# Column sums of the first weights from a column of ones behind a slab of raw x, and one product moved from VectorE to GpSimd

**Chip, cores, metric.** One core of one Trainium2 chip. The metric is the time of the kernel on the device in microseconds (us), median of several executions. The span of the profile is about 1.8 us shorter than the reported time of the same execution. In each call of the experiments one execution of the kernel before lay well above its others (206.99, 205.27, 204.94 and 204.81 us). Only the first, over 1.5% above the fastest, is left out of the ratios; the other three widen their intervals and make the ratios of those calls about 0.1% lower than the medians would.

## The reference

```python
x  = A_x                                  # 1 x 2048 x 640, bf16
xn = layernorm(x)                         # over the 640 columns, no affine part
s  = irfft2(rfft2(xn) * (w_r + 1j*w_i))   # spectral filter, to bf16
g  = silu((gelu(xn @ w_gate) * (xn @ w_up)) @ w_down)   # 640 -> 1536 -> 640
return x + s * g
```

## The kernel before

The kernel does not write its instructions in a fixed order. It collects tasks, each with engines it may run on, a cost, a rank and what it comes after, and a list scheduler of its own ("the plan") runs through them on estimated times. The order in which the plan starts tasks is the order in which they are put on the queue of each engine. Each engine then works through its queue strictly in order, whatever the real times are.

```python
# the plan: when a task may start (cut)
for s in t.new:                     # t needs a free buffer of this tag
    mine = self.slots[s.tag]
    k = len(mine) - self.bufs[s.tag] + ...
    if k >= 0:
        for u in mine[k].users:
            if u.done is None:
                return None
            at = max(at, u.done + self.MARGIN[e])       # MARGIN: PE 250 ns, others 60

BUFS = dict(sp=2, pg=2, pu=2, ..., mc=2, Y=1, R=2, IU=2, ..., xr=3, ...)   # slots per tag
```

TensorE must start before the row statistics of the layer norm are there. So the first two tiles of gate and up work on raw x, turned slab by slab (a slab is 128 rows), and are corrected later: (x - m) r W = r (x W - m colsum(W)). This needs the column sums of the first weights. Before, they are 20 matmuls against a column of ones:

```python
def turn_raw(n1):                       # slabs 0..3 of raw x
    ...                                 # five 128x128 transposes on TensorE, then a copy:
    raw[n1] = add(lambda e: copy_on(e, XR[:, :, n1 * P:(n1 + 1) * P], ...),
                  {"ACT": c_act(640), "DVE": (415, 560)}, ...)
    if n1 < 2:
        k, w, got = ((0, Wg, g_in), (1, Wu, u_in))[n1]
        def sums(e, t):
            for c in range(5):
                nc.tensor.matmul(pt.tile[:, 1, 256 + t:257 + t], lhsT=w[:, c, t*P:t*P+P], rhs=ones, ...)
        ss = [add(..., "PE", (132, 370), (0, 4, k, t), after=[got[t], raw[n1]], ...) for t in range(2)]
        sums_out[k] = add(... copy to WSUM[:, 2*k:2*k+2] ...)

# the corrections of the first two tiles, when RB (row statistics, broadcast to all partitions) has landed
m = add(... nc.vector.scalar_tensor_tensor(out=ev, in0=RB[:, 1], scalar=WSUM[...], in1=ev, mult, add) ...)
normed.append(add(... nc.vector.tensor_tensor(out=ev, in0=ev, in1=RB[:, 0], op=mult) ...))
a = add(gelu of the gate tile, "ACT", ...)
u_done = add(product of both, "DVE", ...)
```

Three other parts matter, none of which the change edits:

```python
def turn_dma(n1, ap):                   # slabs 4..15 of normalised x: a DMA transpose on SyncE's queue
    turned[n1] = add(nc.sync.dma_start_transpose(out=xnT[...], in_=sxn...), "SP", ..., rank (0, 0, n1))

def fold(j, aps):                       # first transform of slabs 2j, 2j+1
    ..., A = ..., Slot("mc")            # only two buffers of this tag
    # two casts PSUM -> A (ScalarE or VectorE), then a store on SyncE's queue:
    stored[j] = dma(D2[:, 2*j:2*j+2, :], A, ...)

def load_res(n1):                       # x again, for the residual at the very end
    nc.gpsimd.dma_start(out=xr_slot, in_=xv[:, n1, :])   # on GpSimd's own queue; three slots
```

Of the kernel before, what the change touches and what calls it, by code (L numbers as in the profile page):

```python
# [11 lines left out]
FP32 = mybir.dt.float32  # L12
# [102 lines left out]
class Plan:  # L115
# [21 lines left out]
    def ready(self, t, e, now):  # L137
# [8 lines left out]
        for s in t.new:  # L146
            mine = self.slots[s.tag]
            k = len(mine) - self.bufs[s.tag] + more.get(s.tag, 0)
            more[s.tag] = more.get(s.tag, 0) + 1
            if k >= 0:  # L150
                for u in mine[k].users:
                    if u.done is None:
                        return None
                    at = max(at, u.done + self.MARGIN[e])
# [68 lines left out]
def kernel(  # L223
# [37 lines left out]
    ones = consts.tile([P, 1], BF16)  # L261
    WSUM = consts.tile([P, 4], FP32)
    XR = persist.tile([P, 5, 512], BF16)
# [89 lines left out]
    nc.gpsimd.memset(ones, 1.0)  # L353
# [101 lines left out]
    def turn_raw(n1):  # L455
        pt = Slot("sp")

        def half():
            return pt.tile[:, 0, :].bitcast(BF16)[:, 0:D]
# [6 lines left out]
        if n1 == 0:  # L466
            keep_warm(2, [a], (0, 0, 0))
        raw[n1] = add(lambda e: copy_on(e, XR[:, :, n1 * P:(n1 + 1) * P], half().rearrange("p (c n) -> p c n", c=5)),
                      {"ACT": c_act(640), "DVE": (415, 560)}, None, (0, n1), after=[a], use=[pt], hold=200)
        if n1 < 2:  # L470
            k, w, got = ((0, Wg, g_in), (1, Wu, u_in))[n1]

            def sums(e, t):
                for c in range(5):
                    nc.tensor.matmul(pt.tile[:, 1, 256 + t:257 + t], lhsT=w[:, c, t * P:t * P + P], rhs=ones, start=(c == 0), stop=(c == 4), skip_group_check=True)
            ss = [add(lambda e, t=t: sums(e, t), "PE", (132, 370), (0, 4, k, t), after=[got[t], raw[n1]], use=[pt]) for t in range(2)]
            sums_out[k] = add(lambda e: copy_on(e, WSUM[:, 2 * k:2 * k + 2], pt.tile[:, 1, 256:258]), {"ACT": c_act(2), "DVE": c_dve(2, 1, True)}, None, (0, -1), after=ss, use=[pt])
# [96 lines left out]
    t = add(rows_pe, "PE", (215, 460), (0, 7), after=[*minused] + [roots[n1] for n1 in range(4)], new=[sr])  # L574
    t = add(lambda e: nc.vector.tensor_copy(out=place(rt, (P,), FP32)[0:8, :], in_=sr.tile[0:8, 0, 0:P]), "DVE", c_dve(128, 1, True), (1, 3, 0.7), after=[t], new=[rt], use=[sr])
# [305 lines left out]
    def gate_up(grp, t):  # L881
# [4 lines left out]
        for k, (w, ps, wt) in enumerate(((Wg, pg, g_in[t]), (Wu, pu, u_in[t]))):  # L886
            parts = [(128 * j, 128 * j + 128) for j in range(4)] if grp == 0 and t < 3 else [(0, 512)]
            mm = []
            for lo, hi in parts:
                def go(e, w=w, ps=ps, lo=lo, hi=hi):  # L890
                    if lo == 0:
                        place(ps, (512,))
                    for c in range(5):
                        nc.tensor.matmul(ps.tile[:, lo:hi], lhsT=w[:, c, t * P:(t + 1) * P],  # L894
                                         rhs=XR[:, c, lo:hi] if early else xnT[:, c, grp * 512 + lo:grp * 512 + hi], start=(c == 0), stop=(c == 4),
                                         skip_group_check=True)
# [4 lines left out]
                              after=[wt] + mm[-1:] + [got[n] for n in range((grp * 512 + lo) // P, (grp * 512 + hi) // P)],  # L901
                              new=[ps] if lo == 0 else [], use=[] if lo == 0 else [ps]))
            last[id(w)] = mm[-1]
# [16 lines left out]
        for k, (w, ps) in enumerate(((Wg, pg), (Wu, pu))):  # L920
# [4 lines left out]
                                                                         op0=ALU.mult, op1=ALU.add), "DVE", c_dve(512, 1), (0, 100), after=[out, rb_in, sums_out[k]], use=[ev])  # L925
            normed.append(add(lambda e, ev=ev: nc.vector.tensor_tensor(out=four(ev), in0=four(ev), in1=RB[:, 0], op=ALU.mult), "DVE", c_dve(512, 1), (0, 100), after=[m], use=[ev]))
# [128 lines left out]
```

## Time and profile before

| | before |
|---|---|
| median of 6 runs (range) | 202.90 us (202.82 to 203.20) |
| span of the profile | 201.2 us |
| TensorE busy | 195.1 us (97%) |
| TensorE's last matmul starts | 197.04 us |
| GpSimd busy | 32.1 us |

The busy shares and the chain stand in the prediction below. First SyncE's queue of the kernel before, in the timeline (start in us, time to issue, engine, line, operation, tiles), then ScalarE's casts of the last two folds in the same stretch. SyncE only issues; the transfer lands later.

```profile
48.84 0.54 SPq L304 DMA_DIRECT2D D<-mc  x1
49.47 1.24 SPq L505 DMA_TRANSPOSE xnT<-s  x1
50.77 0.57 SPq L304 DMA_DIRECT2D T<-tab_t  x1
...
53.12 0.69 ACT L297 CAST mc<-sp 128x640 bf16<-128x640 f32 x1
54.25 0.69 ACT L297 CAST mc<-sp 128x640 bf16<-128x640 f32 x1 [0.44 <-PE sp L542]
```

The first line is the store of the sixth fold: it goes ahead of the last DMA transpose and of a table of 512 KB (T). By the last of its sixteen completions in the trace it lands at 51.55. The last fold's casts need the same mc buffer; they start at 53.12 and wait for nothing but TensorE.

Second, ScalarE at the second corrected tile: the activation of a streamed gate tile (`ge<-pg`) stands ahead of the one of the corrected tile (`ge<-IU`).

```profile
36.50 0.58 ACT L907 ACTIVATE ge<-pg 128x512 bf16<-128x512 f32 x1
36.97 0.62 ACT L907 ACTIVATE ge<-IU 128x512 bf16<-128x512 f32 x1
```

### The profile page before, as it was taken

How to read it: one execution, taken by the hardware profiler on the slowest of the kernel's cores; microseconds unless marked ns; L12 is line 12 of the kernel's file. 1: busy time of each engine (PE TensorE's matmuls, PEld its weight loads, DVE VectorE, ACT ScalarE, POOL GpSimd, SP SyncE). 2: the span in 40 equal slices, each digit the busy share in tenths (PEclk: the TensorE clock that was granted, in tenths of full speed). 3: DMA queues.
4: the chain of work that ended last, by engine and by line, in shares of the span. 5: the costliest groups of instructions: out<-in, count | busy, mean ns of one | idle time of the engine just before them, and what ended most of it. 6: DMA issues, size and time to landing. Idle time of an engine off the chain costs nothing.

```text
span 201.2 us, 4145 instructions
## 1 busy us (share of the span) xinstructions
PE 195.1 (97%) x1530; PEld 118.2 (59%) x1547; DVE 147.7 (73%) x314; ACT 128.9 (64%) x230; POOL 32.1 (16%) x70
## 2 busy tenths in 40 slices
PE   7999999999999999999999999999999999999992
PEld 3994444677544555677755555467765555457781
DVE  3579879999323249999998999933257788888774
ACT  3999699965632768778775766333466565766421
POOL 2413133699100000000000000000001122211210
PEclk9999999999999999999999999999999999999999
DMA  6999999798994947865244210116701243332422
GB/s 175 327 315 324 342 388 213 157 140 201 161 320 152 367 125 158 214 143 190 61 128 122 77 47 21 65 49 224 317 0 47 86 129 103 101 104 92 134 99 65
DMA packets 35894, 32.62 MB, mean 162 GB/s; under 512 B 10910, under 2 KB 32930, under 8 KB 35874
## 3 DMA queue, kind: packets, MB, share of 16 engines
q1 hardware_dynamic: 34434, 29.49, 50.6%
q0 software_dynamic: 1152, 2.66, 6.1%
q10 hardware_dynamic: 288, 0.20, 0.5%
q8 instruction: 12, 0.20, 0.4%
q14 instruction: 8, 0.07, 0.1%
HBM read 22.51 MB, written 9.19 MB: 158 GB/s over the span
## 4 chain that ended last, share of the span: by engine, by line
PE 94%; DMA 2%; ACT 1%; issue 1%; DVE 1%; SPq 0%; DVEq 0%
PE pu L894 26%; PE pg L894 25%; PE pg L972 13%; PE pu L972 13%; PE sp L706 3%; PE sp L839 3%; PE sp L781 2%; PE sp L815 2%; DMA X<-in_A_x_dram 2%; PE sp L541 2%; PE sp L679 2%; PE sp L699 1%; PE sp L833 1%; PE sp L487 1%; PE sp L542 0%
## 5 line engine op out<-in xcount | busy, mean ns | idle before, releaser
L894 PE MATMUL pu<-xnT,Wu 128*128 128x512 bf16 (+1 forms) x237 | 56.7, 365 | 0.5
L894 PE MATMUL pg<-xnT,Wg 128*128 128x512 bf16 (+1 forms) x236 | 56.3, 365 | 0.4
L911 DVE TENSOR_TENSOR uT<-pu,ge 128x512 bf16<-128x512 f32 x46 | 31.7, 690 | 21.9 <-PE pu L894 18.3
L972 PEld LDWEIGHTS <-uT 128*128 128x128 bf16 x396 | 37.9, 98 | 13.5
L907 ACT ACTIVATE ge<-pg 128x512 bf16<-128x512 f32 x46 | 27.5, 598 | 24.4 <-PE pg L894 23.5
L894 PEld LDWEIGHTS <-Wg 128*128 128x128 bf16 x285 | 25.1, 98 | 22.4 <-issue 0.2
L894 PEld LDWEIGHTS <-Wu 128*128 128x128 bf16 x285 | 25.0, 98 | 21.8
L972 PE MATMUL pg<-Wd,uT 128*128 128x320 bf16 (+2 forms) x204 | 30.7, 293 | 0.0
L935 POOL DMA_DIRECT2D xr<-in_A_x_dram x16 | 8.8, 549 | 133.8 <-DVE res L959 133.8
L297 ACT CAST ma<-sp 128x644 bf16<-128x644 f32 (+1 forms) x32 | 23.4, 792 | 9.7 <-PE sp L839 7.9
L972 PE MATMUL pu<-Wd,uT 128*128 128x320 bf16 (+1 forms) x192 | 29.5, 297 | 0.0
L981 ACT ACTIVATE th<-pu 128x320 f32<-128x320 f32 (+1 forms) x16 | 7.0, 435 | 10.7 <-PE pu L972 10.1
L297 ACT CAST IU<-sp 128x640 bf16<-128x640 f32 x16 | 10.9, 691 | 4.2 <-PE sp L781 4.1
L297 ACT CAST Vt<-sp 128x640 bf16<-128x640 f32 x16 | 10.8, 691 | 3.7 <-PE sp L815 3.7
L981 ACT ACTIVATE th<-pg 128x320 f32<-128x320 f32 (+2 forms) x17 | 7.3, 430 | 9.2 <-PE pg L972 8.5
L986 DVE SCALAR_TENSOR_TENSOR G<-th,pg 128x320 bf16<-128x320 f32 (+1 forms) x16 | 7.7, 480 | 7.1 <-ACT th L981 7.1
L986 DVE SCALAR_TENSOR_TENSOR G<-th,pu 128x320 bf16<-128x320 f32 (+1 forms) x16 | 7.7, 480 | 5.4 <-ACT th L981 5.1
L297 ACT CAST mc<-sp 128x640 bf16<-128x640 f32 x16 | 10.6, 703 | 1.3 <-PE sp L542 1.3
L434 POOL TENSOR_TENSOR RSTD<-MVA,mh 128x1 f32<-128x1 f32 x12 | 8.9, 743 | 6.6 <-DVE MVA L416 5.9
L419 ACT ACTIVATE th<-X 128x640 bf16<-128x640 bf16 x11 | 8.1, 738 | 1.6 <-DMA D<-th 1.6
L857 DVE TENSOR_TENSOR mb<-ma 128x640 bf16<-128x640 bf16 x8 | 3.9, 492 | 7.0 <-ACT ma L297 7.0
L759 DVE TENSOR_TENSOR R<-Y 64x644 bf16<-64x644 bf16 x16 | 7.8, 490 | 0.4
(107 smaller groups left out, 246.6 us busy)
## 6 DMA issues: line engine op xcount, KB each, us to landing
BU<-D SPq DMA_DIRECT2D x8, 640.0 KB
D<-mc SPq DMA_DIRECT2D x8, 320.0 KB
xr<-in_A_x_dram POOLq DMA_DIRECT2D x16, 160.0 KB, 2.7
D<-IU SPq DMA_DIRECT2D x8, 320.0 KB
out_dram<-res SPq DMA_DIRECT2D x15, 160.0 KB
Wg<-in_B_w_gate_dram SPq DMA_DIRECT2D x6, 320.0 KB
Wu<-in_B_w_up_dram SPq DMA_DIRECT2D x6, 320.0 KB
Wd<-in_B_w_down_dram SPq DMA_DIRECT2D x6, 320.0 KB
```

The source lines that it names most:

```text
L297: return nc.scalar.copy(out=out, in_=in_) if e == "ACT" else nc.vector.tensor_copy(out=out, in_=in_)
L419: nc.scalar.activation(out=place(junk, (D,)), in_=x, func=ACT.Copy, scale=-1.0 / D, accum_out=less)
L434: nc.gpsimd.tensor_tensor(out=rstd, in0=var, in1=mh, op=ALU.pow)
L706: nc.tensor.matmul(into(q, ri), lhsT=sZ.tile[:, q, ri, :], rhs=FM[:, kinds[q][2] + (4 if ri and kind == 0 else 0), :], start=False, stop=T ...
L759: nc.vector.tensor_tensor(out=o, in0=Yf[:, ::-3, :], in1=Yf[:, 1:3, :], op=ALU.subtract)
L894: nc.tensor.matmul(ps.tile[:, lo:hi], lhsT=w[:, c, t * P:(t + 1) * P], rhs=XR[:, c, lo:hi] if early else xnT[:, c, grp * 512 + lo:grp * 51 ...
L907: nc.scalar.activation(out=ge.tile, in_=pg.tile if src is None else src, func=ACT.Gelu_apprx_tanh)
L911: nc.vector.tensor_tensor(out=u.tile, in0=pu.tile if src is None else src, in1=ge.tile, op=ALU.mult)
L935: nc.gpsimd.dma_start(out=sx.tile, in_=xv[:, n1, :])
L972: nc.tensor.matmul(ps.tile[:, 0:hi - lo], lhsT=uT[grp, ks[i]].tile[:, j * P:(j + 1) * P], rhs=Wd[:, ks[i], lo:hi], start=(i == 0), stop=(i ...
L981: nc.scalar.activation(out=th.tile[:, 0:hi - lo], in_=ps.tile[:, 0:hi - lo], func=ACT.Tanh, scale=0.5)
L986: nc.vector.scalar_tensor_tensor(out=G2.tile[:, lo:hi], in0=th.tile[:, 0:hi - lo], scalar=1.0, in1=ps.tile[:, 0:hi - lo], op0=ALU.add, op1 ...
```

## The change

The intent: no matmuls of their own for the column sums. A column of ones stands in the turned x, behind slab 0, so the matmuls of slab 0 are one column wider and yield the sums in column 128 of pg and pu. With it, VectorE gives the second product of the up corrections to GpSimd, the row statistics are fetched with a higher rank, the plan's rule for buffers handed on within TensorE becomes less cautious, and the plan holds ScalarE free longer for the copy of slab 1 (`hold`, 1000 ns in place of 200). Line numbers shift: L894 becomes L886, L972 L968, L297 L296, L304 L303, L505 L496, L907 L903, L911 L907, L924 L920, L926 L922.

```diff
@@ the plan @@
-                    at = max(at, u.done + self.MARGIN[e])
+                    at = max(at, u.start + u.engs[e][0] if u.on == e == 'PE' else u.done + (self.MARGIN[e] if now > 9000 else 60))
@@ tiles @@
-    ones = consts.tile([P, 1], BF16)
-    XR = persist.tile([P, 5, 512], BF16)
+    XR = persist.tile([P, 5, 513], BF16)
-    nc.gpsimd.memset(ones, 1.0)
+    nc.gpsimd.memset(XR[:, :, 128:129], 1.0)
@@ turn_raw: the sums go, the copies of slabs 0 and 1 stay on ScalarE @@
-        raw[n1] = add(lambda e: copy_on(e, XR[:, :, n1 * P:(n1 + 1) * P], ...
+        raw[n1] = add(lambda e: copy_on(e, XR[:, :, n1 * P + (n1 > 0):(n1 + 1) * P + (n1 > 0)], ...
-                      {"ACT": c_act(640), "DVE": (415, 560)}, ..., hold=200)
+                      {"ACT": c_act(640)} if n1 < 2 else {"ACT": c_act(640), "DVE": (415, 560)}, ..., hold={1: 1000}.get(n1, 200))
-        if n1 < 2:
-            ... (the 20 one-column matmuls and their two copies)
@@ rows (statistics of slabs 0 to 3 on their way to RB) @@
-    t = add(rows_pe, "PE", (215, 460), (0, 7), after=[*minused] + [...], new=[sr])
+    t = add(rows_pe, "PE", (215, 460), (0, 7), after=[*minused, turned[2]] + [...], new=[sr])
-    ... "DVE", c_dve(128, 1, True), (1, 3, 0.7), after=[t] ...
+    ... "DVE", c_dve(128, 1, True), (0, 3.5), after=[t] ...
@@ gate_up, first two tiles @@
-                        nc.tensor.matmul(ps.tile[:, lo:hi], lhsT=..., rhs=XR[:, c, lo:hi] if early else ...
+                        more = early and lo == 0
+                        nc.tensor.matmul(ps.tile[:, lo:hi + more], lhsT=..., rhs=XR[:, c, lo + (lo > 0):hi + 1 if lo or more else hi] if early else ...
+                if early and lo == 0:
+                    sums_out[k, t] = add(... copy_on(e, WSUM[:, 2 * k + t:2 * k + t + 1], ps.tile[:, 128:129]), {"DVE": ...}, ...)
+                    mm.append(sums_out[k, t])
@@ corrections @@
-            normed.append(add(... nc.vector.tensor_tensor(out=four(ev), in0=four(ev), in1=RB[:, 0], op=ALU.mult), "DVE", ...
+            normed.append(add(... (nc.gpsimd if e == "POOL" else nc.vector).tensor_tensor(...), *(("POOL", (1700, 1800), (1, 8)) if k else ("DVE", ...)) ...
```

More of the change, by code (lines that the diff above doesn't have):

```diff
@@ L467, in turn_raw @@
             keep_warm(2, [a], (0, 0, 0))
-        raw[n1] = add(lambda e: copy_on(e, XR[:, :, n1 * P:(n1 + 1) * P], half().rearrange("p (c n) -> p c n", c=5)),
-                      {"ACT": c_act(640), "DVE": (415, 560)}, None, (0, n1), after=[a], use=[pt], hold=200)
-        if n1 < 2:
-            k, w, got = ((0, Wg, g_in), (1, Wu, u_in))[n1]
-            def sums(e, t):
-                for c in range(5):
-                    nc.tensor.matmul(pt.tile[:, 1, 256 + t:257 + t], lhsT=w[:, c, t * P:t * P + P], rhs=ones, start=(c == 0), stop=(c == 4), skip_group_check=True)
-            ss = [add(lambda e, t=t: sums(e, t), "PE", (132, 370), (0, 4, k, t), after=[got[t], raw[n1]], use=[pt]) for t in range(2)]
-            sums_out[k] = add(lambda e: copy_on(e, WSUM[:, 2 * k:2 * k + 2], pt.tile[:, 1, 256:258]), {"ACT": c_act(2), "DVE": c_dve(2, 1, True)}, None, (0, -1), after=ss, use=[pt])
+        raw[n1] = add(lambda e: copy_on(e, XR[:, :, n1 * P + (n1 > 0):(n1 + 1) * P + (n1 > 0)], half().rearrange("p (c n) -> p c n", c=5)),
+                      {"ACT": c_act(640)} if n1 < 2 else {"ACT": c_act(640), "DVE": (415, 560)}, None, (0, n1), after=[a], use=[pt], hold={1: 1000}.get(n1, 200))
     for n1 in range(4):
@@ L573, in rows_pe @@
         nc.tensor.transpose(out=place(sr, (2, 512))[0:8, 0, 0:P], in_=RM.rearrange("p k n -> p (k n)"), identity=identF)
-    t = add(rows_pe, "PE", (215, 460), (0, 7), after=[*minused] + [roots[n1] for n1 in range(4)], new=[sr])
-    t = add(lambda e: nc.vector.tensor_copy(out=place(rt, (P,), FP32)[0:8, :], in_=sr.tile[0:8, 0, 0:P]), "DVE", c_dve(128, 1, True), (1, 3, 0.7), after=[t], new=[rt], use=[sr])
+    t = add(rows_pe, "PE", (215, 460), (0, 7), after=[*minused, turned[2]] + [roots[n1] for n1 in range(4)], new=[sr])
+    t = add(lambda e: nc.vector.tensor_copy(out=place(rt, (P,), FP32)[0:8, :], in_=sr.tile[0:8, 0, 0:P]), "DVE", c_dve(128, 1, True), (0, 3.5), after=[t], new=[rt], use=[sr])
     rs = dma(D5, lambda: rt.tile[0:8, :], (0, -5, 0), 4096, after=[t], use=[rt])
@@ L893, in go @@
                     for c in range(5):
-                        nc.tensor.matmul(ps.tile[:, lo:hi], lhsT=w[:, c, t * P:(t + 1) * P],
-                                         rhs=XR[:, c, lo:hi] if early else xnT[:, c, grp * 512 + lo:grp * 512 + hi], start=(c == 0), stop=(c == 4),
+                        more = early and lo == 0
+                        nc.tensor.matmul(ps.tile[:, lo:hi + more], lhsT=w[:, c, t * P:(t + 1) * P],
+                                         rhs=XR[:, c, lo + (lo > 0):hi + 1 if lo or more else hi] if early else xnT[:, c, grp * 512 + lo:grp * 512 + hi], start=(c == 0), stop=(c == 4),
                                          skip_group_check=True)
@@ L900, in gate_up @@
                 mm.append(add(go, "PE", c_pe(*[hi - lo] * 5), rk,
-                              after=[wt] + mm[-1:] + [got[n] for n in range((grp * 512 + lo) // P, (grp * 512 + hi) // P)],
+                              after=[wt] + mm[-2:] + [got[n] for n in range((grp * 512 + lo) // P, (grp * 512 + hi) // P)],
                               new=[ps] if lo == 0 else [], use=[] if lo == 0 else [ps]))
+                if early and lo == 0:
+                    sums_out[k, t] = add(lambda e, k=k, ps=ps: copy_on(e, WSUM[:, 2 * k + t:2 * k + t + 1], ps.tile[:, 128:129]),
+                                         {"DVE": c_dve(1, 1, True)}, None, (0, -1), after=[mm[-1]], use=[ps])
+                    mm.append(sums_out[k, t])
             last[id(w)] = mm[-1]
@@ L924, in gate_up @@
             m = add(lambda e, ev=ev, k=k: nc.vector.scalar_tensor_tensor(out=four(ev), in0=RB[:, 1], scalar=WSUM[:, 2 * k + t:2 * k + t + 1], in1=four(ev),
-                                                                         op0=ALU.mult, op1=ALU.add), "DVE", c_dve(512, 1), (0, 100), after=[out, rb_in, sums_out[k]], use=[ev])
-            normed.append(add(lambda e, ev=ev: nc.vector.tensor_tensor(out=four(ev), in0=four(ev), in1=RB[:, 0], op=ALU.mult), "DVE", c_dve(512, 1), (0, 100), after=[m], use=[ev]))
+                                                                         op0=ALU.mult, op1=ALU.add), "DVE", c_dve(512, 1), (0, 100), after=[out, rb_in, sums_out[k, t]], use=[ev])
+            normed.append(add(lambda e, ev=ev: (nc.gpsimd if e == "POOL" else nc.vector).tensor_tensor(out=four(ev), in0=four(ev), in1=RB[:, 0], op=ALU.mult), *(("POOL", (1700, 1800), (1, 8)) if k else ("DVE", c_dve(512, 1), (0, 100))), after=[m], use=[ev]))
         a = add(lambda e: act(e, evs[0].tile), "ACT", c_act(512), (0, 100), after=normed[:1], new=[ge], use=evs[:1])
```

## The prediction

> **What bounds the kernel now.** I read the page's busy shares first, then the chain of work that ended last, then busy time by stretch, and last the order of instructions in the first 8 us and around 30 to 40 us, which is all that the change touches.
>
> ```profile
> PE 195.1 (97%) x1530; PEld 118.2 (59%) x1547; DVE 147.7 (73%) x314; ACT 128.9 (64%) x230; POOL 32.1 (16%) x70
> ...
> PE 94%; DMA 2%; ACT 1%; issue 1%; DVE 1%; SPq 0%; DVEq 0%
> ```
>
> TensorE (PE) is busy for 195.1 of the 201.2 us span, and the chain is TensorE for 94%. So I ask of each part of the change only: does it take time from TensorE's stream, or open a gap in it? In which stretch, the next view says (after the count of the window: busy us and instructions of each engine, then clock, DMA share, GB/s).
>
> ```profile
> 5.26:7.30 2.04, 1.94 (x41) 1.82 (x40) 0.65 (x2) 2.04 (x5) 0.64 (x2) 1.00 1.10 321
> 7.30:12.60 5.30, 5.30 (x101) 5.30 (x99) 3.74 (x11) 5.05 (x13) 2.23 (x6) 1.00 1.16 326
> 12.60:40.00 27.40, 27.30 (x174) 14.71 (x173) 24.88 (x56) 25.51 (x59) 9.88 (x19) 1.00 1.06 288
> ```
>
> From 7.30 us on the first column has no room: 5.30 of 5.30 and 27.30 of 27.40. I also took every start-to-start distance of the matmuls and subtracted N/2.4 ns. After 7 us the only excess over 100 ns that is not a missing record (those are all 218 ns, one 512-column matmul) is 121 ns at 39.38 us. TensorE streams from 7 us to its last matmul at 197.0 us, and the 4.2 us after that are a tail of ScalarE, VectorE and one store. So the time is: when TensorE starts to stream, plus its work, plus the tail. The change can only touch the first two. The stretch in question:
>
> ```profile
> 4.28 1.06 PE L369 MATMUL sp<-uT 128*128 128x512 bf16 x2
> ...
> 5.26 0.27 PE L475 MATMUL sp<-ones,Wg 128*128 128x1 bf16 x5
> ...
> 5.40 0.60 PE L464 MATMUL sp<-ident,X 128*128 128x128 bf16 x5
> ...
> 5.83 0.27 PE L475 MATMUL sp<-ones,Wg 128*128 128x1 bf16 x5
> ...
> 5.96 1.25 PE L894 MATMUL pg<-XR,Wg 128*128 128x128 bf16 x15
> 6.03 0.69 ACT L297 COPY XR<-sp 128x640 bf16<-128x640 bf16 x1
> ...
> 7.05 0.39 PE L475 MATMUL sp<-ones,Wu 128*128 128x1 bf16 x10
> ...
> 7.31 0.44 PE L464 MATMUL sp<-ident,X 128*128 128x128 bf16 x5
> ```
>
> The second number is duration, and matmuls overlap, so I read starts: the ten one-column matmuls of Wu hold TensorE from 7.05 to 7.31, 25.4 ns each. The fifteen matmuls at 5.96 hide a gap: the last five of them start only at 6.78, when the ScalarE copy of slab 1 (6.03 + 0.69 = 6.72) is done; TensorE stood still for 0.26 us. There are 0.13 us more ahead of 5.26. By the last of the sixteen completions of each transfer, slab 1 of x landed at 5.21, the first Wu at 6.60, slab 2 at 7.07, slab 3 at 7.55.
>
> **What the Trainium skill says.** "TensorE: Matmul & The Clock Gate", section "Wait — 56ns, not 53.3ns?": a matmul takes N/1.2 ns cold, N/2.4 + 2.5 ns warm, and never less than about 25 ns from start to start. The trace agrees: 25.4 ns for one column, 56 for 128, and 107 for the cold transposes before 5.8 us. A column more in a 128-column matmul is therefore 0.4 ns; a matmul of its own is 25. "PSUM — Partial Sum Buffer", section "PSUM bank collisions raise a hardware error": TensorE must not write a bank while another engine reads it. So the copy of a sum out of the bank of pg or pu holds up the next slab's matmuls into that bank. The kernel before shows no such wait (its sums had a bank of their own). "GPSIMD Engine Reference", section "3.1 Elementwise — side-by-side cycle accounting": a two-input fp32 product is 1.96 times VectorE's at 2048 elements. The trace before has no GpSimd product of this size. "SBUF — State Buffer", section "Who interferes with whom": GpSimd reading SBUF contends with a VectorE instruction of two SBUF inputs, and one blocks the other whole. The trace fits: GpSimd's 128x1 power takes 0.55 us in calm stretches and 2.24 us at 40.57 us, amid back-to-back VectorE tensor_tensors.
>
> **The change part by part.**
> 1. Removed: 20 one-column matmuls with their weight loads. Starts: 5.264 to 5.396, 5.833 to 5.961, 7.052 to 7.306, that is 0.132 + 0.128 + 0.254 = 0.51 us of TensorE. Added: one column in 20 matmuls, 20 x 0.42 ns = 0.01 us.
> 2. How much of the 0.51 us is gained? The 0.254 us of the Wu sums stand after the last gap, in the stream: all of it. The 0.26 us of the Wg sums stand ahead of the gap that ends at 6.78. That end is set by slab 1's copy, which follows slab 1's transposes, which follow its landing at 5.21 at the cold clock; I let the copy end where it did, so the removal would only widen the gap. But the first Wu is there at 6.60, and its slab 0 products can now go first, at about 6.66 in place of 6.78: 0.12 us. Gain 0.25 + 0.12 = 0.37 us.
> 3. Moved: two ScalarE copies of the sums (0.164 us each by the view of that tile) become four on VectorE of one column each; by the 0.15 us of its smallest instruction (L416) some 0.6 us. VectorE is busy for only 0.65 of 2.04 and 3.74 of 5.30 us here, so that is not the bound.
> 4. Added wait: matmul, sum copy, next matmul of the same bank. A matmul shows 0.22 us; ScalarE began 0.04 us after the last transpose's end (4.485 to 4.52), and TensorE 0.06 us after a copy's end (6.72 to 6.78). With a 0.15 us copy: 0.22 + 0.04 + 0.15 + 0.06 = 0.47 us between the starts, where a free stream has 0.06. Four times 0.41 us would be 1.6 us if nothing stood between. The plan knows of the dependence and has transposes and the other three banks' slabs to put there, 0.28 us each, so most is filled. I charge 0.1 us, for a VectorE queue in which a statistics instruction (0.45 us) that waits for a landing stands ahead of a copy.
> 5. GpSimd takes the last up product. Here are the four instructions of the corrections (durations are minimum, median, maximum):
>
> ```profile
> L924 DVE SCALAR_TENSOR_TENSOR IU<-RB,WSUM,IU x2: 743/744/746, 29.8 to 34.1; 128x512 f32<-128x512 f32 x2
> L924 DVE SCALAR_TENSOR_TENSOR R<-RB,WSUM,R x2: 743/744/745, 30.4 to 34.8; 128x512 f32<-128x512 f32 x2
> L926 DVE TENSOR_TENSOR IU<-IU,RB x2: 679/680/681, 31.7 to 36.0; 128x512 f32<-128x512 f32 x2
> L926 DVE TENSOR_TENSOR R<-R,RB x2: 681/682/684, 32.3 to 36.6; 128x512 f32<-128x512 f32 x2
> ```
>
> VectorE loses 2 x 0.68 us; GpSimd gains 2 x 1.34 us by the page's ratio (an estimate; the plan books 1.7). The results are wanted by the down product's second half: its matmuls start at 39.94 us, and the last corrected tile is ready at 38.92 (38.24 + 0.68). That is 1.0 us of slack against 0.66 to 1.0 us more latency, and the row statistics are now fetched with more urgency: before, their broadcast landed at 29.43 and the first correction ran at 29.78. I expect that fetch about 1 us earlier and no gap. Zero.
> 6. The plan's rule for buffers reused within TensorE, and its smaller margin early on, change the order only. In a stream without gaps that is worth zero.
>
> Sum: -0.25 - 0.12 + 0.01 + 0.10 = -0.26 us. From 202.86 that is 202.6; since some of the retuning may close part of the 0.39 us of early gaps, I take 202.5.
>
> **The rivals.**
> - The sum copy's round trip becomes the wait. For it: four new links from TensorE to VectorE and back, each 0.41 us if bare. Against: VectorE is half idle there. If half of it shows: +0.8 - 0.4, 203.3 us.
> - GpSimd is blocked by VectorE's two-input instructions (12.60 to 40 us: 24.88 of 27.40 us busy) and the down product waits. For it: the 2.24 us power. Against: the earlier fetch, and the wait takes two products in turn, not one. With 2 us per product: about +1 us, 203.5.
> - The odd offset of slabs 1 to 3 in the widened tile slows reading by TensorE or writing by VectorE. No run here shows it either way. If 60 matmuls of 128 columns took twice as long: 60 x 56 ns = 3.4 us, 206. I give that 2%.
> - The whole 0.51 us and the early gaps of 0.39 us are won: 201.95.
>
> **Range and chances.** The best case adds up to 0.9 us and the likely losses to 0.8, so 201.8 to 203.2. Faster by over 2% would take 4.1 us from a stream that holds only 0.5 us of removable work: 1%. Slower by as much needs the third rival: 2%.
>
> **What would show it.** TensorE's last matmul starts 0.2 to 0.5 us before 197.04; no one-column matmuls; the 128-column ones at 56 ns still; the Wu products of slab 0 start near 6.66; no TensorE gap over 0.1 us between 7.3 and 13 us, nor at 36 to 41; GpSimd's products between 1.3 and 2 us; the tail at 4.2 us. A gap ahead of a slab 1 product that ends with a WSUM copy would prove the first rival, one ahead of the second half of the down product the second, start distances over 60 ns the third.

## The result, and the profile after

| | before | after |
|---|---|---|
| median of 6 runs (range) | 202.90 us (202.82 to 203.20) | 204.15 us (203.08 to 204.46) |
| ratio, 95% interval | | 1.0052 (1.0029 to 1.0076) |
| span of the profile | 201.2 us | 202.6 us |
| TensorE busy | 195.1 us | 195.1 us |
| last matmul starts | 197.04 us | 198.40 us |

A ratio here is the mean time of one kernel's runs over that of the other's of the same rounds, so not quite the ratio of the medians. The kernel became 0.5% slower: "within 2%" was right, the range (up to 203.2) was not. The page of the kernel after, its busy shares and its chain:

```profile
PE 195.1 (96%) x1509; PEld 117.9 (58%) x1527; DVE 149.6 (74%) x320; ACT 127.0 (63%) x224; POOL 33.0 (16%) x72
...
PE 92%; DMA 4%; issue 1%; ACT 1%; DVE 1%; DVEq 0%; ACTq 0%
```

Against the same lines of before: 21 matmul records fewer (20 of them the sums), and DMA went from 2% to 4% of the chain. The list of groups says which DMA, in its last two columns (idle time before the group, and what ended most of it). First two groups of the kernel before, then the same two after:

```profile
L894 PE MATMUL pg<-xnT,Wg 128*128 128x512 bf16 (+1 forms) x236 | 56.3, 365 | 0.4
...
L297 ACT CAST mc<-sp 128x640 bf16<-128x640 f32 x16 | 10.6, 703 | 1.3 <-PE sp L542 1.3
```

```profile
L886 PE MATMUL pg<-xnT,Wg 128*128 128x512 bf16 (+1 forms) x235 | 56.2, 365 | 1.8 <-ACT ge L903 1.4
...
L296 ACT CAST mc<-sp 128x640 bf16<-128x640 f32 x15 | 9.8, 694 | 6.1 <-DMA D<-mc 4.8
```

Now TensorE waits 1.4 us for a gelu on ScalarE, and ScalarE waits 4.8 us for a store. The timeline of the kernel after shows how they hang together (SyncE, ScalarE, TensorE):

```profile
47.29 0.57 SPq L303 DMA_DIRECT2D T<-tab_t  x1
47.95 2.55 SPq L496 DMA_TRANSPOSE xnT<-s  x2
50.60 0.55 SPq L303 DMA_DIRECT2D D<-mc  x1
...
57.88 1.29 ACT L296 CAST mc<-sp 128x640 bf16<-128x640 f32 x2 [4.82 <-DMA D<-mc]
59.06 1.11 ACT L903 ACTIVATE ge<-pg 128x512 bf16<-128x512 f32 x2
...
59.72 1.24 PE L886 MATMUL pg<-xnT,Wg 128*128 128x512 bf16 x5 [1.35 <-ACT ge L903]
```

The order of SyncE's queue has changed: the sixth fold's store now stands behind the table and two DMA transposes. It lands at 57.81 instead of 51.55. Because mc has two buffers, the last fold's cast waits for it; ScalarE works in order, so the gelus behind that cast wait too; both pg banks fill up, and TensorE stops at 58.2. Nothing in the diff mentions any of these instructions.

To see where TensorE's time went I took the start-to-start distances of its matmuls minus N/2.4 ns and summed them over stretches (records that are missing, each 218 ns, made equal). This table is the ledger for all that follows; it has three of the experiments too, and the moment from which the clock record of the trace has the full clock (matmuls of 128 columns then take 56 instead of 107 ns):

| us of excess in | before | after | xr_late | store_early | stats_first |
|---|---|---|---|---|---|
| 0 to 10 | 3.17 | 2.85 | 2.51 | 2.44 | 2.44 |
| 30 to 40 | 0.27 | 0.42 | 0.96 | 1.00 | 0.14 |
| 50 to 60 | 0.34 | 1.84 | 0.34 | 0.34 | 0.33 |
| last matmul starts | 197.04 | 198.40 | 197.07 | 197.05 | 196.16 |
| full clock from | 5.8 | 6.4 | 3.9 | 5.3 | 4.8 |

All other stretches agree within 0.05 us in sum. So after against before: -0.32 + 0.15 + 1.50 = +1.33, and the last matmul moved by +1.36. The change gained early, lost half of it at 30 to 40 us, and lost 1.50 us at 58 to 60.

### The profile page after: what moved, and what is told of

It is laid out like the page before. It is cut to its first block, busy times and chain, and to the rows that moved or that the text cites. A ratio compares the mean times of both kernels' runs of the same rounds, so it can differ in the third digit from the quotient of the medians.

```text
span 202.6 us, 4105 instructions
## 1 busy us (share of the span) xinstructions
PE 195.1 (96%) x1509; PEld 117.9 (58%) x1527; DVE 149.6 (74%) x320; ACT 127.0 (63%) x224; POOL 33.0 (16%) x72
## 4 chain that ended last, share of the span: by engine, by line
PE 92%; DMA 4%; issue 1%; ACT 1%; DVE 1%; DVEq 0%; ACTq 0%
PE pu L886 24%; PE pg L886 23%; PE pg L968 13%; PE pu L968 12%; DMA D<-mc 4%; PE sp L697 3%; PE sp L830 3%; PE sp L772 2%; PE sp L806 2%; PE sp L368 2%; PE sp L670 2%; PE sp L532 1%; PE sp L690 1%; PE sp L824 1%; PE sp L463 1%
## 5 line engine op out<-in xcount | busy, mean ns | idle before, releaser
L886 PE MATMUL pg<-xnT,Wg 128*128 128x512 bf16 (+1 forms) x235 | 56.2, 365 | 1.8 <-ACT ge L903 1.4
L886 PE MATMUL pu<-xnT,Wu 128*128 128x512 bf16 (+1 forms) x237 | 57.2, 365 | 0.5
L907 DVE TENSOR_TENSOR uT<-pu,ge 128x512 bf16<-128x512 f32 x46 | 31.6, 689 | 22.6 <-PE pu L886 15.3
L968 PEld LDWEIGHTS <-uT 128*128 128x128 bf16 x396 | 37.8, 98 | 13.6
L903 ACT ACTIVATE ge<-pg 128x512 bf16<-128x512 f32 x46 | 27.3, 597 | 23.3 <-PE pg L886 22.4
L886 PEld LDWEIGHTS <-Wg 128*128 128x128 bf16 x285 | 25.5, 99 | 23.6 <-issue 1.6
L886 PEld LDWEIGHTS <-Wu 128*128 128x128 bf16 x285 | 25.1, 98 | 21.8
L968 PE MATMUL pg<-Wd,uT 128*128 128x320 bf16 (+2 forms) x204 | 30.5, 293 | 0.0
L968 PE MATMUL pu<-Wd,uT 128*128 128x320 bf16 (+1 forms) x192 | 29.7, 297 | 0.0
L296 ACT CAST ma<-sp 128x644 bf16<-128x644 f32 (+1 forms) x32 | 23.4, 793 | 9.7 <-PE sp L830 7.9
L296 ACT CAST mc<-sp 128x640 bf16<-128x640 f32 x15 | 9.8, 694 | 6.1 <-DMA D<-mc 4.8
L296 ACT CAST IU<-sp 128x640 bf16<-128x640 f32 x16 | 10.9, 691 | 4.2 <-PE sp L772 4.1
L296 ACT CAST Vt<-sp 128x640 bf16<-128x640 f32 x16 | 10.8, 691 | 3.7 <-PE sp L806 3.7
```

Of the source, the lines that this page charges most:

```text
L296: return nc.scalar.copy(out=out, in_=in_) if e == "ACT" else nc.vector.tensor_copy(out=out, in_=in_)
L886: nc.tensor.matmul(ps.tile[:, lo:hi + more], lhsT=w[:, c, t * P:(t + 1) * P], rhs=XR[:, c, lo + (lo > 0):hi + 1 if lo or more else hi] if ...
L903: nc.scalar.activation(out=ge.tile, in_=pg.tile if src is None else src, func=ACT.Gelu_apprx_tanh)
L907: nc.vector.tensor_tensor(out=u.tile, in0=pu.tile if src is None else src, in1=ge.tile, op=ALU.mult)
L968: nc.tensor.matmul(ps.tile[:, 0:hi - lo], lhsT=uT[grp, ks[i]].tile[:, j * P:(j + 1) * P], rhs=Wd[:, ks[i], lo:hi], start=(i == 0), stop=(i ...
```

## The experiments

Four calls, each with its own runs of the kernel before on the same chip; their medians were 203.04, 203.11, 203.05 and 203.10 us. My theory after reading the traces was the chain above. Rivals: the place in the queue alone does it; the GpSimd product does it, by holding VectorE; the sums' copies do it. "The sixth store" is `stored[5]`.

### Only the order of SyncE's queue

Two kernels with the store moved after the plan has run; nothing else differs. In store_late it goes, in the kernel **before**, behind the next DMA on SyncE's queue, a transpose:

```diff
-        for t in plan.run():
+        seqd = plan.run()
+        s5 = stored[5]; i = seqd.index(s5)
+        k = next(j for j in range(i + 1, len(seqd)) if seqd[j].on == "SP")
+        seqd.insert(k + 1, s5); del seqd[i]
+        for t in seqd:
             t.emit(t.on)
```

> The kernel before with one instruction moved: the sixth store of the first transform (D2) goes behind the next DMA transpose in the SyncE queue; nothing else changes. Theory (the 1.5 us in the changed kernel come from that store landing late, so that ScalarE waits for its buffer and TensorE then waits for ScalarE): the store lands near 57 us instead of 51.6, ScalarE waits 4 to 5 us for it, TensorE stands still 1.0 to 2.0 us near 58 to 60 us, time 203.9 to 204.9. Rival (the 1.5 us come from the new sums, the GpSimd products or the new positions in XR, not from the queue): no TensorE gap near 58 us, 202.7 to 203.1.

Measured: 203.01 us (202.82 to 203.20), ratio 0.9997 (0.9983 to 1.0010). A miss. The store landed at 53.95 and ScalarE hardly waited:

```profile
54.03 1.29 ACT L297 CAST mc<-sp 128x640 bf16<-128x640 f32 x2 [0.96 <-DMA D<-mc]
```

Both last transposes had landed by 52.67 in this run, against 56.76 in the kernel before and 57.01 after. So a place behind a transpose is not enough; the transposes have to be late themselves.

In store_early the store goes, in the kernel **after**, right behind its last cast, which puts it ahead of one of the two transposes:

```diff
-        for t in plan.run():
+        seqd = plan.run()
+        s5 = stored[5]; seqd.remove(s5)
+        seqd.insert(max(seqd.index(a) for a in s5.after) + 1, s5)
+        for t in seqd:
             t.emit(t.on)
```

> The changed kernel with the same store moved forward, to right behind its last copy; it then stands ahead of one of the transposes that it stood behind, all other orders the same. Theory: it lands near 54 us instead of 57.8, the ScalarE wait falls from 4.8 to 1 to 2.5 us, the TensorE gap of 1.5 us goes or falls below 0.3 us, time 202.5 to 203.1. Rival: the gap and 204.1 us stay.

Measured: 202.83 us (202.75 to 203.00), ratio 0.9988 (0.9976 to 1.0000). The store landed at 54.13, the stop at 58 us is gone, and with it the whole loss. So the late store is what costs the time.

### Only the buffer

spare_buffer lets the last fold of the kernel after cast into the slot "Y", which is idle then, so no store has to land first. The order of the queues stays.

```diff
-        sxn, eo, xf, A = xn_of[j], Slot("ma"), Slot("mb"), Slot("mc")
+        sxn, eo, xf, A = xn_of[j], Slot("ma"), Slot("mb"), Slot("Y" if j == 7 else "mc")
```

> The changed kernel with another buffer (one that lies idle until later) for the last pair of slabs in place of the third user of a double buffer, so that no copy waits for the store at all. Theory: no ScalarE wait for the store, no TensorE gap near 58 us; the early gain minus the loss at 37 to 38 us is left, 0.1 to 0.3 us under the kernel before: 202.5 to 202.8. Rival: a gap of over 1 us stays somewhere between 50 and 62 us, 203.8 to 204.3.

Measured: 202.96 us (202.80 to 203.87), ratio 1.0001 (0.9984 to 1.0018). No stop at 58. The profiled execution was the slowest, of 203.87: the stores still landed late there (the sixth at 59.41), and what reads them stopped TensorE eight microseconds on:

```profile
66.81 1.07 PE L670 MATMUL sp<-T,BU 128*128 128x128 bf16 x16 [0.89 <-DMA BU<-D]
```

The buffer carried the wait to TensorE at 58; freeing it leaves the lateness itself. So the question became why the transposes and the store are so late.

### What makes the transfers late: the residual's loads

In the kernels before and after, three loads of x for the residual (`xr`, 160 KB each, on GpSimd's queue) are issued at 48.7 to 50.4 us, though nothing needs them before some 150 us. They run right beside the DMA transposes. In the trace the transposes move in packets of 256 bytes and these loads in packets of 5120; one such packet took 196 to 201 ns (median) in store_late and store_early, where the two hardly met, but 278 ns after, 412 in spare_buffer and 487 before. The profile's windows, after the count of the stretch: busy time and instructions of each engine, then TensorE's clock, the DMA engines' busy share and GB/s. From 53 to 56 us, first the kernel after:

```profile
53.00:56.00 3.00, 3.00 (x15) 1.37 (x14) 0.69 (x1) 0.07 (x1) 0.00 (x0) 1.00 1.08 161
```

then store_early:

```profile
53.00:56.00 3.00, 3.00 (x17) 1.35 (x16) 0.69 (x1) 2.01 (x4) 0.00 (x0) 1.00 1.15 288
```

About the same busy share of the DMA engines moved 161 GB/s in the one and 288 in the other. That is a correlation, so I held the loads back. xr_late is the kernel after with one column of each of the first three slots written by GpSimd first, from a table (TI) that lands at about 78 us; the load must wait for that write.

```diff
             place(sx, (D,))
+            if n1 < 3:
+                nc.gpsimd.tensor_copy(out=sx.tile[:, 0:1], in_=TI[:, 0, 0:1])
             nc.gpsimd.dma_start(out=sx.tile, in_=xv[:, n1, :])
```

> The changed kernel, all orders kept, but the first three loads of x for the residual on the GpSimd queue wait (through a one-column copy of the TI table) until about 80 us; they are used at 150 us. Theory now: the store is late because the transposes ahead of it crawl while they share the DMA engines with those three loads (packets of the loads 280 to 490 ns, transposes 40 to 60 KB per us); without them the transposes land by 54 us, the sixth store by 55, ScalarE waits under 2 us, no TensorE gap near 58 us nor at 66 us: 202.5 to 202.9 us. Rival (the table and two transposes ahead in the queue are enough by themselves): store at 56 us or later, a gap of about 1 us, 203.6 to 204.3.

Measured: 203.01 us (202.63 to 203.24), ratio 0.9986 (0.9954 to 1.0018). The order of SyncE's queue is that of the kernel after, store behind two transposes, yet:

```profile
50.78 0.53 SPq L303 DMA_DIRECT2D D<-mc  x1
...
53.99 1.29 ACT L296 CAST mc<-sp 128x640 bf16<-128x640 f32 x2 [0.73 <-DMA D<-mc]
```

Transposes landed at 52.75 and 53.06, the store at 53.91 instead of 57.81, and TensorE did not stop. In the profiled executions, then, it takes both: the place in the queue, and the loads beside it. The kernel before with the same edit, as a control:

> The kernel before with the same three loads held back. Theory: its transposes also land sooner (last one near 53 us in place of 56.8), but TensorE never waited for them, so no change: 202.7 to 203.1. Rival (those loads cost something in the kernel before too): under 202.5.

Measured: 203.01 us (202.78 to 203.22), ratio 0.9987 (0.9955 to 1.0019). Its last transpose landed at 52.55 instead of 56.76, and the time did not move. The kernel before has the collision too, but its store is ahead of it, so nobody waits.

### Parts of the change alone

sums_alone is the kernel before with the sums part only: the widened XR, the one-column WSUM copies, slabs 0 and 1 on ScalarE. Rule, ranks and product as before.

```diff
 (kernel after, with these three undone)
-  at = max(at, u.start + u.engs[e][0] if u.on == e == 'PE' else ...)
+  at = max(at, u.done + self.MARGIN[e])
-  rows: after=[*minused, turned[2]] ... (0, 3.5)
+  rows: after=[*minused] ...            (1, 3, 0.7)
-  up product on "POOL"
+  up product on "DVE"
```

> The kernel before with the sums part alone (ones column, sums out of pg and pu, copies on VectorE, slabs 0 and 1 raised by ScalarE); no GpSimd product, no earlier fetch of the row statistics, the old rule for buffer reuse. Theory: TensorE loses 0.1 to 0.2 us more in gaps before 8 us and saves 0.51 us of matmuls, net 0.3 to 0.4 us ahead at 12 to 30 us; but in its plan the sixth store stands behind all transposes, as in store_late, so a gap of 0.8 to 2 us near 58 us: 203.3 to 204.5. Rival (the sums themselves make the change slow): the gap shows in the first 13 us, and none near 58 us.

Measured: 203.95 us (203.50 to 204.76), ratio 1.0047 (1.0025 to 1.0068). About the loss of the whole change, but not in the way expected: the sixth store landed at 52.20 and there is no stop at 58, so the time fell into the expected range by luck. The profiled execution, of 203.65 us, was 0.62 us ahead in the ledger's first row (2.55), and then the order that the plan made out of the changed tasks has small gaps of its own: 0.25 at 13.5, 0.14 at 14.2, 0.31 at 32.9, 0.20 at 39.6. Its last matmul starts at 197.29, only 0.25 us after that of the kernel before; the other 0.44 us of its longer span come after the last store has landed (more on this under stats_first). The slower executions, up to 204.76, were not profiled, so most of this loss stays open. The order of the whole change does not have these gaps; which of its other parts removes them was not tried.

product_alone is the kernel before with the up product on GpSimd, and nothing else:

```diff
-            normed.append(add(... nc.vector.tensor_tensor(...), "DVE", c_dve(512, 1), (0, 100), ...))
+            normed.append(add(... (nc.gpsimd if e == "POOL" else nc.vector).tensor_tensor(...), *(("POOL", (1700, 1800), (1, 8)) if k else ("DVE", ...)), ...))
```

> The kernel before with the GpSimd products alone. Theory: GpSimd holds VectorE's two-input instructions up, 0.2 to 0.8 us of TensorE gaps at 35 to 41 us against 0.12, and in its plan the sixth store stands ahead of the table, so none near 58 us: 203.0 to 203.7. Rival (the relief of VectorE pays): 202.6 to 202.8.

Measured: 205.39 us (204.02 to 205.77), ratio 1.0081 (1.0037 to 1.0125), above the range of the theory. TensorE's waits in two stretches of this kernel (in all, times, longest), 30 to 46 us and 60 to 70 us:

```profile
PE sp L541 <- DVE mb L528: 0.9, 1, 0.9
...
PE sp L679 <- DMA BU<-D: 1.5, 1, 1.5
```

The second is the lateness of the stores again, in another kernel, with a transpose landing at 57.29. product_xr_late holds the loads back in it:

> product_alone with the residual loads held back. Theory: the 1.62 us gap at 66.5 us goes (the stores of the first transform landed late there behind transposes that crawled beside those loads), the 1.05 us gap at 38.8 us stays (VectorE held up by GpSimd): 203.7 to 204.2 against 205.4. Rival (the gap at 66.5 us comes with the product's plan, whatever the loads do): 205.2 or more.

Measured: 204.10 us (203.73 to 204.31), ratio 1.0041 (1.0009 to 1.0073). The wait for BU is gone, transposes and store landed by 53.33, and the median is 1.3 us lower. The wait for VectorE's `mb` stayed, at 38.90, 1.05 us. That confirms the collision in a kernel other than the one in which I had found it.

Is the product a loss in the change as a whole? xr_late_dve is xr_late with the product put back on VectorE after planning (same order of every queue but VectorE's and GpSimd's):

```diff
-            normed.append(add(... (nc.gpsimd if e == "POOL" else nc.vector).tensor_tensor(...
+            normed.append(add(... nc.vector.tensor_tensor(...
```

> As xr_late, and the two up products that GpSimd does are put out on VectorE, at the places where the plan has them. Theory: the gaps at 36 to 39 us (0.25 us in the changed kernel, 0.83 in store_early) come from VectorE instructions that GpSimd's products block (1.38 us in place of 0.74); they go back to 0.1 to 0.2 us and the time is 0.1 to 0.4 us under xr_late: 202.3 to 202.7. Rival (VectorE needs the relief): VectorE is later by 1.4 us, gaps of 0.5 us or more at 36 to 40 us, 0.2 to 0.6 us over xr_late.

Measured: 202.90 us (202.74 to 203.11), ratio 0.9982 (0.9950 to 1.0013); last matmul at 196.99 against 197.07. The gaps at 36 to 39 us stayed (0.69 us in the ledger's second row, 0.96 in xr_late), so they do not come from the product, as the theory had it; nor did the rival's loss of time appear. In this order the product on GpSimd gains nothing and loses nothing beyond the noise.

### Why 202.8 to 203.0 and not 202.5: a gap at 36 to 39 us

Without the collision, the ledger's second row stays: xr_late and store_early begin 0.66 and 0.73 us better than before and give 0.7 us back between 36 and 39. The gap that ends before the third group of the down product ended 7.8 us after the first correction in each kernel: 29.64 and 37.42 (after), 29.78 and 37.58 (store_early), 29.82 and 37.60 (xr_late). The first correction waits for the broadcast RB of the row statistics. So I suspected an anchor: however far ahead TensorE is, it stops there until the statistics have come through. The trace of the kernel after has the way between, on VectorE and ScalarE:

```profile
29.64 0.75 DVE L920 SCALAR_TENSOR_TENSOR IU<-RB,WSUM,IU 128x512 f32<-128x512 f32 x1 [0.66 <-DMA RB<-D]
...
35.45 0.63 ACT L903 ACTIVATE ge<-IU 128x512 bf16<-128x512 f32 x1 [1.12 <-DVE IU L922]
...
36.80 0.57 ACT L903 ACTIVATE ge<-pg 128x512 bf16<-128x512 f32 x1
```

In the kernel before, the `ge<-pg` stands ahead of this `ge<-IU`; now it stands behind it. It frees a bank of pg when it ends, at 37.37, and the third group of the down product needs that bank: it starts at 37.42. The order of a second queue, ScalarE's, had changed. That this order is the link is read from the traces; no run puts the two gelus back.

To test the anchor I tried to move the broadcast. First attempt, on top of xr_late: issue it on GpSimd's queue instead of SyncE's.

```diff
     rb_in = dma(RB..., D5...partition_broadcast(P), (0, -5, 1), 524288, after=[rs])
+    rb_in.emit = lambda e: nc.gpsimd.dma_start(out=RB..., in_=D5...partition_broadcast(P))
```

> xr_late with one more transfer moved: the broadcast of the row statistics (RB) goes out on the GpSimd queue, where it does not stand behind the weights of the down product; all orders else as in xr_late. Theory: the lead that the sums give (0.3 us at 30 us) is lost because the first correction waits for that broadcast (29.6 to 29.8 us in every run so far) and the down product starts its third group a fixed 7.78 us after it; the broadcast now lands before 28 us, VectorE does not wait for it, the gaps at 36 to 39 us fall from 0.8 to under 0.3 us, last matmul 0.3 to 0.6 us before 197.04, time 202.4 to 202.8, 0.2 to 0.6 us under the kernel before. Rival (the gap comes from GpSimd's products holding VectorE): the gap stays, 202.9 to 203.1.

> stats_free with the two up products on VectorE instead of GpSimd. If GpSimd's products pay nothing, because VectorE is blocked for as long as it is relieved (0.64 + 0.48 us against 2 x 0.68): the same as stats_free within 0.15 us. If they cost: 0.2 us or more faster; if they pay: 0.2 us or more slower.

> The kernel before with both transfers moved (the residual loads held, the broadcast on the GpSimd queue). TensorE has one gap of 0.12 us to lose there: 202.7 to 203.1, no more than 0.15 us under the kernel before. If it falls as far as stats_free, the sums are not what pays there.

Measured: 203.47 us (203.11 to 203.73), ratio 1.0010 (0.9979 to 1.0042); with the product on VectorE 203.34 (202.56 to 203.64), ratio 1.0000 (0.9967 to 1.0033); in the kernel before 203.67 (203.35 to 204.00), ratio 1.0023 (0.9991 to 1.0055). stats_free and the kernel before lie above their expected ranges. Inconclusive: the first corrections of the first two came at 29.23 and 29.91, at most 0.6 us earlier than in xr_late. In the trace of stats_free the second row is down to 0.14, but its clock rose only at 7.1 us and its first row is 3.16, so there was no lead to give back.

Second attempt, on top of xr_late: move the broadcast within SyncE's queue, ahead of two loads of the down weights (stats_first), or behind one more (stats_later).

```diff
-        for t in plan.run():
+        seqd = plan.run()
+        seqd.remove(rb_in)
+        seqd.insert(seqd.index(d_in[2]), rb_in)         # stats_first
+        # seqd.insert(seqd.index(d_in[6]) + 1, rb_in)   # stats_later
+        for t in seqd:
             t.emit(t.on)
```

> The other direction: the broadcast behind one more weight load. Theory: it lands about 0.8 us later, first correction near 30.5, gap in front of the third group of the down product at 7.78 us after it, last matmul near 197.8, time 203.5 to 204.0. Rival: no change from xr_late, 202.9 to 203.1.

> xr_late with the broadcast of the row statistics moved ahead of two weight loads of the down product in the SyncE queue; all other orders kept. Theory (the lead of the sums is taken back because the first correction waits for that broadcast, and the third group of the down product follows the correction at 7.78 us): the broadcast lands 1 to 1.7 us sooner, the first correction starts at 28.4 to 29.0 us, the gaps at 36 to 39 us fall below 0.4 us together, last matmul at 196.3 to 196.8, time 202.3 to 202.8. Rival (the gaps have another cause, so the end at 197.0 us is the sums' fault): the gaps stay at 0.5 to 0.8 us and the last matmul at 197.0.

Measured, stats_later: 204.49 us (204.39 to 205.50), ratio 1.0072 (1.0042 to 1.0102). The broadcast slipped further than expected, and the third group followed it (the profiled execution was the slowest, of 205.50):

```profile
32.34 0.75 DVE L920 SCALAR_TENSOR_TENSOR IU<-RB,WSUM,IU 128x512 f32<-128x512 f32 x1 [3.46 <-DMA RB<-D]
...
40.12 0.97 PE L970 MATMUL pg<-Wd,uT 128*128 128x320 bf16 x6 [0.38 <-ACT ge L903]
```

40.12 - 32.34 = 7.78, as before. Measured, stats_first: 202.86 us (202.51 to 203.62), ratio 0.9992 (0.9959 to 1.0025).

```profile
28.46 0.74 DVE L920 SCALAR_TENSOR_TENSOR IU<-RB,WSUM,IU 128x512 f32<-128x512 f32 x1
...
36.88 0.98 PE L970 MATMUL pg<-Wd,uT 128*128 128x320 bf16 x6
```

Here the third group came 8.42 us after the first correction: no longer held, and the ledger's second row is 0.14. The last matmul starts at 196.16, 0.88 us ahead of the kernel before. The traces show the anchor in both directions; of the times, only those of stats_later are clear of the noise.

Only half of the 0.88 us reaches the span (200.74 us against 201.18). The last store lands 3.2 us after that matmul starts in both kernels, but the engines' closing synchronisation ends 4.58 us after it in place of 4.14. The traces of sums_alone, stats_first_dve and before_stats_first have the same 0.44 us more, those of the three stats_free kernels 0.24.

The six times fall in two groups, 202.51, 202.52, 202.54 and 203.17, 203.23, 203.62; the profiled execution was of the first. The same with the product on VectorE, and the same broadcast moved in the kernel before (there ahead of all loads of the down weights, with held loads):

> stats_first with the two up products on VectorE. If GpSimd's products are worth nothing, within 0.15 us of stats_first; if they cost, 0.2 us or more under it; if they pay, 0.2 us or more over it.

> The kernel before with the residual loads held and the broadcast moved ahead of the weight loads in the same way. It has at most 0.12 us of gaps to lose at 36 to 40 us: 202.8 to 203.1. If it gets as fast as stats_first, the sums do not pay even where nothing takes their lead back.

Measured: 202.85 us (202.68 to 203.46), ratio 0.9988 (0.9960 to 1.0016), no gap at 36 to 39 either; in the kernel before 203.93 (203.80 to 204.22), ratio 1.0039 (1.0012 to 1.0066): slower, since the moved broadcast pushes a store back and ScalarE's cast waits 2.1 us for it. What helps one order harms another.

The two groups of times have a likely cause in the first microseconds. The profiled execution of stats_first (202.51 us), then that of stats_first_dve (203.46 us), TensorE's second slab:

```profile
5.26 0.44 PE L463 MATMUL sp<-ident,X 128*128 128x128 bf16 x5
```

```profile
5.32 0.71 PE L463 MATMUL sp<-ident,X 128*128 128x128 bf16 x5
```

The same five transposes take 0.44 and 0.71 us: the clock was at full speed in the one, and rose only at 6.7 us in the other. Over the profiles the rise lay between 3.9 and 7.1 us. In the orders of the changed kernel the ledger's first row goes with it: 2.44 to 2.51 us with a rise at 3.9 to 5.3, 2.68 to 2.76 at 5.8 to 6.3, 2.85 and 2.86 at 6.4, 3.00 at 6.7, 3.16 at 7.1. The kernel before and its variants have 2.99 to 3.29 whenever it rose (4.3 to 6.7). A kernel held by an anchor hides this (xr_late and xr_late_dve, with the rise at 3.9 and 6.0, start the last matmul at 197.07 and 196.99); stats_first does not (196.16, and stats_first_dve 196.98). That the slow group of stats_first had late clocks was not profiled and stays open.

No kernel beats the one before beyond doubt: the best medians, 202.83 to 202.90, come with intervals that reach or include 1.

## Why the prediction was right or wrong

**1, removal of the sums: right.** No one-column matmuls, and the wider ones at 55 to 59 ns from start to start once the clock is full.

**2, the early gain of 0.37 us: right in size, wrong in what fills the gap.** TensorE in the kernel after, first 8 us:

```profile
5.82 1.00 PE L886 MATMUL pg<-XR,Wg 128*128 128x129 bf16 x10
6.66 0.44 PE L478 MATMUL sp<-ident,s 128*128 128x128 bf16 x5
6.94 0.45 PE L886 MATMUL pg<-XR,Wg 128*128 128x128 bf16 x5
7.22 0.27 PE L886 MATMUL pu<-XR,Wu 128*128 128x129 bf16 x2
```

The gap that ended at 6.78 is closed, though not by the products that I named: a normalised slab is turned at 6.66, and the Wu products of slab 0 start at 7.22. The ledger has 0.32 us, with a clock that rose 0.6 us later than in the profile before; xr_late_dve, whose clock rose at 6.0, has 0.49. In the traces this gain goes with the moment of the clock's rise, as listed above; the prediction left that out.

**3 and 4, the sums' copies: right.** VectorE took 0.16 and 0.15 us for such a copy, and no TensorE gap ends with one. The first rival (+0.4) and the third (odd offset: VectorE's copy to it took 495 ns against 492 before) did not happen.

**5, the GpSimd product: right in duration and in its worth, wrong in its reason.** It took 1.27 and 1.36 us (estimated 1.34, from a ratio that the page measured on an add). But VectorE was held beside it: from the timeline of the kernel after, GpSimd and VectorE,

```profile
32.33 1.27 POOL L922 TENSOR_TENSOR R<-R,RB 128x512 f32<-128x512 f32 x1 [1.09 <-DVE R L920]
32.77 1.38 DVE L920 SCALAR_TENSOR_TENSOR IU<-RB,WSUM,IU 128x512 f32<-128x512 f32 x1
...
35.94 1.16 DVE L907 TENSOR_TENSOR uT<-R,ge 128x512 bf16<-128x512 f32 x1
```

The second and third lines took 0.74 and 0.68 us before. 0.64 + 0.48 = 1.12 us of the 1.36 saved on VectorE were lost again. And the statistics did not arrive about 1 us earlier, as I had assumed: their broadcast was issued 0.88 us earlier (22.28 instead of 23.16), but it landed at 29.61 instead of 29.43, and the first correction moved from 29.78 to 29.64 only.

**6 failed:** "In a stream without gaps that is worth zero." The changed order did matter, though the stream of before had no gaps, because every queue works in order and two of them had changed. Nor did the plan's rule alone change it, as this step had it. With the old rule, sums_alone already has the sixth store behind both transposes (issued at 49.39, the transposes from 46.15 on), and product_alone has the gelu of the corrected tile ahead of the streamed one (35.72 and 37.05). So steps 1 and 5 were priced without the new order that they bring; the rule and the rank were never run alone. And I had read only the first 8 us and 30 to 40 us as what the change touches, while the loss stands at 58 to 60. On SyncE's queue the sixth store came to stand behind two transposes that are slow because of three loads nobody waits for: 1.50 us by the ledger, shown by store_early and xr_late, which remove it in two unrelated ways. On ScalarE's queue a gelu that frees a bank of pg came to stand behind one that waits for the row statistics: 0.15 us here, 0.7 where the early lead is larger. stats_first and stats_later show that the arrival of the statistics sets it; the part of ScalarE's order is read from the traces. None of my rivals was this.

The sum of the other terms, -0.26, is not confirmed by the times: without the late store the kernel comes to 202.83 to 203.01, 0.1 to 0.2 us under the kernel before of the same call, with intervals that reach or include no gain. The traces have the early gain, and the anchor takes it back. The 202.5 of three executions of stats_first was not this change alone: its loads are held back and its broadcast is moved.

What stays open: why the transposes met the loads in some executions and not in others (the kernel after ranged from 203.08 to 204.46; store_late kept its loads and the two hardly met); what the rule and the rank do alone; why the closing synchronisation is 0.24 or 0.44 us longer in some kernels.

## What to carry to other kernels

Where a scheduler decides the order of the queues, a small edit is a new order everywhere, and "only reordering" is to be priced by what each in-order queue now holds up: for each store that frees a buffer, ask which transfers stand ahead of it. Loads that are wanted much later do not belong beside transfers that someone waits for, even on another queue; holding back three of them took 1.1 and 1.3 us off the medians of two kernels. And a gain early in a stream that has a later fixed point, here the arrival of the row statistics, is worth nothing until that point moves too.

## What the Trainium skill lacked or had wrong

- "DMA: Bandwidth & Descriptors", section "SWDGE vs HWDGE vs iDMA", says that loads issued by GpSimd and those issued by SyncE feed different internal queues of each DMA engine, which takes turns between them. It gives no cost of that. Here packets of 5120 bytes on the former beside 256-byte packets of DMA transposes on the latter went from 196 ns to as much as 503 ns (medians; the most in product_alone), and the last transpose landed 7.8 us after its issue (49.25 to 57.01) in place of 3.6 (49.45 to 53.06) with the loads held back.
- "SBUF — State Buffer", section "Who interferes with whom", was right on VectorE and GpSimd but gives no size for this pair: an fp32 product of 512 columns on GpSimd (1.27 and 1.36 us) held two-input VectorE instructions from 0.74 to 1.38 and from 0.68 to 1.16 us.
- "TensorE: Matmul & The Clock Gate", section "Part 1: The HAM clock gate", puts the rise of the clock at about 4 us of work, within 500 ns from run to run. Over the profiles here, with the same warm-up matmuls from 1.21 us on, it lay between 3.9 and 7.1 us after the start, so after 2.7 to 5.9 us of work: wider than those 500 ns either way, though within the free-running window of 3.4 us that the same section gives. It puts the worth of the ramp under 1% of a typical span. That agrees, and is still more than this change could gain: two profiled executions of nearly the same kernel, with the rise at 4.8 and at 6.7 us, took 202.51 and 203.46 us, and 0.56 us of the difference stand in the first 10 us of TensorE (2.44 and 3.00 us of excess).
